# One linear-attention and two-MLP kernel: the product v_m · w per chunk in two half steps, the first chunk's by pairs of batches

## The chip, the core and the metric

The kernel runs on one core of a Trainium2 chip. The metric is the device time of one execution in microseconds (us). Three runs of the kernel before gave 841.07, 841.46 and 845.69 us, a median of 841.46 us.

## What is computed

Four batches of eight heads, 576 positions of 64 dimensions, go through an attention with 32 memory slots, and its output, 2304 rows of 512, through two MLPs:

```python
a = softmax(phi, over positions)               # (B, H, S, 32)
k_m, v_m = a^T k, a^T v                        # (B, H, 32, 64) each
attn = softmax(q k_m^T / 8, over the 32 slots) # (B, H, S, 32)
x = attn v_m                                   # as rows of 512
x = ((x w_a) * (x w_b)) w_out                  # first MLP, 1536 wide
out = elu(x w_in) w_out2                       # second MLP, 2048 wide
```

All data are 32-bit floats; the weights come as 64-bit floats and are turned into pairs of 32-bit parts on the chip.

## The kernel before, in words

**The parts hi and lo.** To keep accuracy, an operand is split into a part hi (rounded, written by ACT) and a part lo (the rest, subtracted by DVE). A product is three matmuls: hi·hi, hi·lo, lo·hi.

**v_m · w.** The kernel never forms x = attn v_m. It multiplies v_m by the first MLP's weights instead: for every chunk f of 128 of the 1536 columns, `step_u(f)` (L459) forms u = v_m·[w_a, w_b]. v_m stands in two tiles, `vthi` and `vtlo` (L254), of 128 partitions by 4 blocks `kc` of (batch, slot) columns. A head is half a column of the array, so two row tiles of 64 rows each (`i` = 0, 1) run side by side; each has its own PSUM tile `u_ps` of two banks. A chunk takes 4 blocks x 3 parts x 2 row tiles = 24 matmuls of 64x256. The columns of the result's partitions are the four batches' 32 slots: one pass gives u for all batches. Then ACT copies each PSUM tile into `ur` (`upper`, L482), DVE subtracts to get the lo part (`lower`, L485), and SP issues 16 transfers (L499) that spread `ur` over the four batches' own tiles `u`. The matmuls that use them are `ab_ps` (`steps_ab`, L617): attn's hi and lo parts `xhi`, `xlo` against u.

**The attention stage.** The loop over batches (L519) issues, for each batch b, in program order: `stage_kv(b, 0, ·)`, the k side (PSUM tile `pk`, L360), `stage_kT`, which copies it to `kt` (L374), `stage_scores(b)` (`sc`, `sl`, L390, L394), `stage_aT(b+1)`, the transposed softmax of the next batch (`tp_a`, L339), `stage_softmax(b)` (L416 to L420), `stage_kv(b, 1, 0)`, `stage_vT(b, 0)` (ACT copies into `vthi` at L380, DVE subtracts into `vtlo` at L382), `stage_norm(b)` (DVE L434 to L436, and a multiply on POOL at L438), `stage_kv(b, 1, 1)`, `stage_vT(b, 1)`. `stage_xT(b-1)` transposes the normalized scores into the PSUM tiles `tp_x` (L449) and `tl_x` (L453) and splits them into `xhi` (L69) and `xlo` (L70). In the last batch the v side goes first, then `stage_xT(2)`, then `step_u(0, 0)`, and only then the k side and the scores of batch 3.

**PSUM.** `pstile` (L61) hands out tiles of two banks from a pool of two during the attention stage; `sc`, `tp_a`, `tp_x` and `u_ps` take them in turn, so each waits until the tile before the last has been read. Later a second pool of two joins. `pone` gives single banks for `pk`, `tl_x` and `sl` from a pool of four.

**Order of the work.** All engines run their instructions in the order in which the program issues them. `step(pe, evac, amount)` (L218) issues one group of matmuls, then `fill(amount)`, then the evacuation, then what earlier steps have deferred by so many steps (`defer`). `fill` issues pieces of the weight conversion, seven DVE operations per unit of 128x512 weights (`piece`, L144: L155, L158, L142, L163, L168, L173, L176), with ACT operations between them (L113, L119, L133); a piece also issues the next unit's load on POOL's DMA queue (L103). SP issues the loads of q, k, v and phi and the 16 transfers of each chunk. Between the attention stage and the first MLP the kernel frees one pool of tiles and opens another; the softmax of batch 3 (L577 to L601) then runs beside the first `ab_ps` steps.

Of the kernel before, what the change touches and what calls it, by code (L numbers as in the profile page):

```python
# [7 lines left out]
F32 = mybir.dt.float32  # L8
F32R = mybir.dt.float32r
# [4 lines left out]
AF = mybir.ActivationFunctionType  # L14
ALU = mybir.AluOpType
# [6 lines left out]
def attention_then_two_mlps(ctx, tc, q, kv, kv_left, phi, w_ab, w_o1, w_i2, w_o2, out):  # L22
# [13 lines left out]
    nc = tc.nc  # L36
    B, P, KC, S = q.shape
# [23 lines left out]
    def pstile(name):  # L61
        turn[0] += 1
        return pss[turn[0] % len(pss)].tile([P, 2, 512], F32, tag="ps", name=name)
# [117 lines left out]
    def weights(key):  # L181

        n = index[key]
        while n in cu:
            assert piece(), key
        return ready[key]

    def drop(key):
        ready.pop(key)
        live[units[index[key]][1]] -= 1  # L190
# [3 lines left out]
    def fill(amount):  # L194
        credit[0] += amount
        while credit[0] >= 1.0:
            credit[0] -= 1.0
            if not piece():
                credit[0] = 0.0
# [10 lines left out]
    def defer(steps, fn, at=2):  # L210

        later.append([steps, fn, at])

    def flush_later():
        while later:
            later.pop(0)[1]()

    def step(pe, evac, amount, order=ORDER):  # L218


        pe()
        for e in later:
            e[0] -= 1
        due = [e for e in later if e[0] <= 0]
        later[:] = [e for e in later if e[0] > 0]
        evac = evac if isinstance(evac, list) else [evac]
        for k in order:
            if k == "f":
                fill(amount / order.count("f"))
            elif k in "abc":  # L230
                if "abc".index(k) < len(evac):
                    evac["abc".index(k)]()
            else:
                for e in due:
                    if e[2] == int(k):
                        e[1]()

    def tick():
        step(lambda: None, [], 0, "012")
# [5 lines left out]
    pu = es_u.enter_context(tc.tile_pool(name="pu", bufs=2, reuse_waits="tile"))  # L245
# [8 lines left out]
    vthi, vtlo = [pa.tile([P, KC, B, M], F32R, name=f"vt{x}") for x in ("hi", "lo")]  # L254
# [30 lines left out]
    for b in range(1, B):  # L285
        first, second = [("kv", b, 0, 0), ("kv", b, 0, 1), ("q", b, 0), ("q", b, 1)], [("kv", b, 1, 0), ("kv", b, 1, 1)]
        if b + 1 == B:
            first, second = second, first
# [63 lines left out]
    def stage_kv(b, n, u):  # L352

        a, t, left = st["a", b], st["kv", b, n, u], st["left", b]
        pk = pone("pk")
        for i in range(2):
            c = i if n == 0 or b % 2 == 0 else 1 - i
            for j in range(NJ + 1):
                rows = t[:, j, c, :] if j < NJ else left[0:LEFT, u, n, c, :]
                nc.tensor.matmul(pk[:, i * P:(i + 1) * P], rows, a[0:P if j < NJ else LEFT, u, j, :],  # L360
                                 start=(j == 0), stop=(j == NJ))
        st["pk", n, b, u] = pk
        more_loads("kv", *(("left",) if n == 1 and u == 1 else ()))

    def own(t, i, straight=True):

        if straight:
            return t[64 * i:64 * i + 64, 0:3 * P].rearrange("p (t s) -> p t s", s=192)[:, :, M * i:M * i + M]
        return t[64 * i:64 * i + 64, 64:192].rearrange("p (t s) -> p t s", s=64)[:, :, M * i:M * i + M]

    def stage_kT(b, u):
        pk = st.pop(("pk", 0, b, u))
        for i in range(2):
            nc.scalar.activation(out=own(kts[u], i), in_=own(pk, i), func=AF.Copy)  # L374

    def stage_vT(b, u):
        pk = st.pop(("pk", 1, b, u))
        hi, lo = [[x[64 * i:64 * i + 64, 2 * u:2 * u + 2, b, :] for i in range(2)] for x in (vthi, vtlo)]
        for i in range(2):
            nc.scalar.activation(out=hi[i], in_=own(pk, i, b % 2 == 0), func=AF.Copy)  # L380
        for i in range(2):
            nc.vector.tensor_tensor(out=lo[i], in0=own(pk, i, b % 2 == 0), in1=hi[i].bitcast(F32), op=ALU.subtract)  # L382
# [73 lines left out]

    u_t, g_t = {}, {}

    def step_u(f, amount):  # L459

        tiles = [pstile("u_ps") for _ in range(2)]

        def pe():
            for kc in range(KC):
                hi, lo = [x[:, (kc % 2) * 256:(kc % 2) * 256 + 256] for x in weights(("ab", f, kc // 2))]
                for n, (v, w) in enumerate(((vthi, hi), (vthi, lo), (vtlo, hi))):
                    for i in range(2):
                        r = slice(64 * i, 64 * i + 64)  # L470
                        nc.tensor.matmul(  # L471
                            tiles[i][:, kc // 2, (kc % 2) * 256:(kc % 2) * 256 + 256],
                            v[r, kc].rearrange("p b m -> p (b m)"), w[r], start=(n == 0), stop=(n == 2),
                        )
            drop(("ab", f, 0))
            drop(("ab", f, 1))

        us = [pu.tile([P, 2, 2, 256], F32R, tag="u", name="u", bufs=5) for _ in range(B)]
        ur = pu.tile([P, 2, KC, 2, 256], F32R, tag="ur", name="ur", bufs=1)

        def upper(i):
            nc.scalar.activation(out=ur[:, i, :, 0], in_=tiles[i].rearrange("p k (c n) -> p (k c) n", c=2), func=AF.Copy)  # L482

        def lower(i):
            nc.vector.tensor_tensor(out=ur[:, i, :, 1], in0=tiles[i].rearrange("p k (c n) -> p (k c) n", c=2),  # L485
                                    in1=ur[:, i, :, 0].bitcast(F32), op=ALU.subtract)

        def second():
            lower(0)
            upper(1)  # L490

        def third():
            lower(1)
            for b in range(B):
                for c in range(2):
                    for i in range(2):
                        o = 64 * c + M * i
                        src = ur[M * b:M * b + M, i].rearrange("p (k c) h n -> p k c (h n)", c=2)[:, :, c ^ (b % 2)]
                        nc.sync.dma_start(out=us[b][o:o + M].rearrange("p k h n -> p k (h n)").bitcast(F32),  # L499
                                          in_=src.bitcast(F32))  # L500

        defer(1, second)
        defer(2, third)
        for b in range(B):
            u_t[f, b] = us[b]
        step(pe, lambda: upper(0), amount)

    with tc.manual_schedule():
        make_identity(nc, ident)
        kts = [p0.tile([P, 3 * P], F32, name=f"kt{i}", bufs=1) for i in range(2)]  # L510
        for t in kts:
            nc.gpsimd.memset(t, 0.0)

        st["ident"] = ident
# [4 lines left out]
        for b in range(B):  # L519
            nxt = b + 1 < B  # L520
            if not nxt:
                stage_kv(b, 1, 0)
                stage_vT(b, 0)
                stage_kv(b, 1, 1)
                stage_vT(b, 1)
                flush_later()
                stage_xT(b - 1)
                step_u(0, 0)
            stage_kv(b, 0, 0)
            if b == 0:  # L530
                stage_kT(b, 0)
                stage_aT(0, (1,))
                stage_kv(b, 0, 1)
                stage_kT(b, 1)
                stage_a(1, 0)
                stage_a(1, 1)
            else:
                if nxt:
                    a_max(b + 1, 0)
                    a_max(b + 1, 1)  # L540
                stage_kT(b, 0)
                if nxt:
                    a_exp(b + 1, 0)
                stage_kv(b, 0, 1)
                stage_kT(b, 1)
                if nxt:
                    a_end(b + 1, 0)
                    a_exp(b + 1, 1)
                    a_end(b + 1, 1)
            if nxt:  # L550
                flush_later()
            else:
                tick()
            if nxt and b:
                stage_xT(b - 1)
            if b == 0:
                magnitude(0)
                low_word(0)
            else:
                fill(FA)  # L560
            stage_scores(b)
            if not nxt:
                tick()
                break
            stage_aT(b + 1)
            soft_tiles(b)
            stage_softmax(b)
            stage_kv(b, 1, 0)
            fill(FB)
            stage_vT(b, 0)  # L570
            stage_norm(b, nc.gpsimd)
            stage_kv(b, 1, 1)
            stage_vT(b, 1)
            fill(FC)


# [241 lines left out]
        for f in range(NF2):  # L818
            for k in range(NB):
                t = (f + k) % NB  # L820
# [63 lines left out]
```

## Time and profile before

| | |
|---|---|
| median of three runs | 841.46 us |
| the profiled execution | 842.81 us, span from first to last instruction 841.0 us |
| PE, matmuls | 818.8 us busy (97%), 5168 instructions |
| DVE | 612.7 us busy (73%), 1015 instructions |
| ACT | 415.0 us busy (49%), 646 instructions |
| POOL | 50.8 us busy (6%) |
| transfers u <- ur on SP's queue | 192, 128 KB each |

The span is the time from the first to the last instruction, and the run's own time contains what lies around it. PE is TensorE's matmuls, PEld its weight loads, DVE VectorE, ACT ScalarE, POOL GpSimd, SP SyncE. In the timelines each row gives start, duration, engine, line, operation, out <- in, count, and in square brackets the idle time of the engine before it with what ended it. Rows merge equal neighbours, so that a row's start is that of its first instruction.

### The profile page before, as it was taken

Reading aid. Unit: us, or ns where it says so; the run is one execution under the profiler, and the core shown is the slowest. Engines: PE = TensorE matmul, PEld = TensorE weight load, DVE = VectorE, ACT = ScalarE, POOL = GpSimd, SP = SyncE. Lnnn points to the kernel's source line nnn. Section 1 sums busy time; section 2 is a strip of 40 time slices with the busy share of each in tenths; the row PEclk is TensorE's granted clock in tenths of the full one; section 3 lists DMA queues with packets and bytes.
Section 4 is the critical chain, followed back from the end, with each engine's and each line's share of the span. In section 5 each row is a group of like instructions: output and inputs, shape, how many; then the busy total and the mean of one; then the engine's idle time right before and its main releaser. Section 6 shows DMA issues by size and latency. Waiting matters only on the chain.

```text
span 841.0 us, 13020 instructions
## 1 busy us (share of the span) xinstructions
PE 818.8 (97%) x5168; PEld 762.3 (91%) x5168; DVE 612.7 (73%) x1015; ACT 415.0 (49%) x646; POOL 50.8 (6%) x88
## 2 busy tenths in 40 slices
PE   5999988999999999999999999999999999999998
PEld 4887888999999999999999898889998889998896
DVE  1886688888997898567788852887777876776555
ACT  2544366664454544333348763565544565543360
POOL 1111200000000000000000000000000000000000
PEclk9998999999999999999999999999999999999999
DMA  9771566655765477416001110111111110100006
GB/s 308 280 272 55 126 151 173 173 136 138 161 157 134 111 175 156 113 55 151 29 2 50 51 51 1 51 51 51 51 51 51 51 50 26 51 26 1 1 0 225
DMA packets 32173, 82.90 MB, mean 99 GB/s; under 512 B 4849, under 2 KB 4849, under 8 KB 32113
## 3 DMA queue, kind: packets, MB, share of 16 engines
q1 hardware_dynamic: 22320, 46.41, 20.4%
q0 software_dynamic: 9792, 35.66, 14.5%
q8 instruction: 41, 0.67, 0.3%
q14 instruction: 20, 0.16, 0.1%
HBM read 52.17 MB, written 4.72 MB: 68 GB/s over the span
## 4 chain that ended last, share of the span: by engine, by line
PE 90%; DVE 5%; DMA 3%; ACT 1%; issue 1%; SPq 1%; DVEq 0%; ACTq 0%
PE o_ps L784 24%; PE h_ps L741 24%; PE o_ps L659 17%; PE ab_ps L617 15%; PE pk L360 5%; PE u_ps L471 2%; PE sc L390 1%; DVE ur L485 1%; DMA kv_t<-in_kv_dram 1%; DMA u<-ur 1%; DMA raw<-in_w_o_dram 1%; SPq L499 1%; DVE a_sb L626 1%; PE tp_a L339 0%; DVE gl L628 0%
## 5 line engine op out<-in xcount | busy, mean ns | idle before, releaser
L617 PE MATMUL ab_ps<-xhi,u 128*128 128x288 f32 x768 | 138.6, 297 | 2.9 <-DVE xlo L70 1.2
L617 PEld LDWEIGHTS ab_ps<-xhi,u 128*128 128x128 f32 x768 | 114.0, 188 | 4.8 <-DVE xlo L70 1.4
L784 PE MATMUL o_ps<-ulh,g2h 128*128 128x512 f32 x288 | 114.1, 396 | 0.0
L784 PE MATMUL o_ps<-ull,g2h 128*128 128x512 f32 x288 | 114.1, 396 | 0.0
L784 PE MATMUL o_ps<-ulh,g2l 128*128 128x512 f32 x288 | 103.4, 396 | 0.0
L759 DVE SCALAR_TENSOR_TENSOR e<-e,th 128x768 f32<-128x768 f32 x48 | 46.0, 959 | 76.2 <-ACT e L756 75.8
L741 PE MATMUL h_ps<-yh,usl 128*128 128x384 f32 x384 | 98.1, 336 | 0.0
L741 PE MATMUL h_ps<-yh,ush 128*128 128x384 f32 x384 | 98.1, 336 | 0.0
L741 PE MATMUL h_ps<-yl,ush 128*128 128x384 f32 x384 | 98.0, 336 | 0.0
L752 ACT ACTIVATE e<-h_ps 128x768 f32<-128x768 f32 x48 | 39.0, 813 | 96.0 <-PE h_ps L741 94.0
L659 PE MATMUL o_ps<-gh,ull 128*128 128x288 f32 x384 | 82.5, 296 | 0.9 <-DVE ull L142 0.9
L659 PE MATMUL o_ps<-gh,ulh 128*128 128x288 f32 x384 | 82.8, 297 | 0.1
L659 PE MATMUL o_ps<-gl,ulh 128*128 128x288 f32 x384 | 82.3, 295 | 0.0
L617 PE MATMUL ab_ps<-xlo,u 128*128 128x288 f32 x384 | 82.2, 296 | 0.0
L741 PEld LDWEIGHTS h_ps<-yh,ush 128*128 128x128 f32 x384 | 69.6, 188 | 1.3
L741 PEld LDWEIGHTS h_ps<-yh,usl 128*128 128x128 f32 x384 | 69.5, 188 | 0.0
L741 PEld LDWEIGHTS h_ps<-yl,ush 128*128 128x128 f32 x384 | 69.5, 188 | 0.0
L784 PEld LDWEIGHTS o_ps<-ulh,g2l 128*128 128x128 f32 x288 | 54.2, 188 | 13.2
L784 PEld LDWEIGHTS o_ps<-ulh,g2h 128*128 128x128 f32 x288 | 54.2, 188 | 12.5
L784 PEld LDWEIGHTS o_ps<-ull,g2h 128*128 128x128 f32 x288 | 54.2, 188 | 12.5
L626 DVE TENSOR_TENSOR a_sb<-a_sb,ab_ps 128x576 f32<-128x576 f32 x48 | 36.1, 752 | 36.5 <-PE ab_ps L617 30.6
L659 PEld LDWEIGHTS o_ps<-gh,ull 128*128 128x128 f32 x384 | 61.5, 188 | 1.1 <-DVE ull L142 1.1
(105 smaller groups left out, 1456.9 us busy)
## 6 DMA issues: line engine op xcount, KB each, us to landing
u<-ur SPq DMA_DIRECT2D x192, 128.0 KB, 4.5
raw<-in_w_o_dram POOLq DMA_DIRECT2D x28, 512.0 KB, 4.0
raw<-in_w_ab_dram POOLq DMA_DIRECT2D x24, 512.0 KB, 5.4
kv_t<-in_kv_dram SPq DMA_DIRECT2D x16, 512.0 KB, 6.6
raw<-in_w_i_dram POOLq DMA_DIRECT2D x16, 512.0 KB, 3.8
q_t<-in_q_dram SPq DMA_DIRECT2D x8, 576.0 KB, 7.2
out_dram<-y SPq DMA_DIRECT2D x8, 512.0 KB, 3.0
phi_t<-in_phi_dram SPq DMA_DIRECT2D x3, 576.0 KB, 4.8
```

Source lines behind the costliest of these rows:

```text
L360: nc.tensor.matmul(pk[:, i * P:(i + 1) * P], rows, a[0:P if j < NJ else LEFT, u, j, :], start=(j == 0), stop=(j == NJ))
L390: nc.tensor.matmul(sc[:, u, j * P:(j + 1) * P], qs[u][:, t, j * P:(j + 1) * P], kts[u][:, t * P:(t + 1) * P], start=(t == 0), stop=(t == 1))
L471: nc.tensor.matmul(tiles[i][:, kc // 2, (kc % 2) * 256:(kc % 2) * 256 + 256], v[r, kc].rearrange("p b m -> p (b m)"), w[r], start=(n == 0) ...
L485: nc.vector.tensor_tensor(out=ur[:, i, :, 1], in0=tiles[i].rearrange("p k (c n) -> p (k c) n", c=2), in1=ur[:, i, :, 0].bitcast(F32), op=A ...
L499: nc.sync.dma_start(out=us[b][o:o + M].rearrange("p k h n -> p k (h n)").bitcast(F32), in_=src.bitcast(F32))
L617: nc.tensor.matmul(ps[:, h, 0:HS], u[:, kk, w, n * P:n * P + P], x[b][:, kk, h * HS:(h + 1) * HS], start=(kk == 0 and i == 0), stop=(kk == ...
L626: nc.vector.tensor_tensor(out=a_sb, in0=a_sb, in1=ps[:, :, 0:HS], op=ALU.mult)
L659: nc.tensor.matmul(ps[:, h, 0:HS], w[:, cc], g[:, h * HS:(h + 1) * HS], start=(n == 0 and i == 0), stop=(n == len(fs) - 1 and i == 2),)
L741: nc.tensor.matmul(ps[:, h, 0:HB], w[:, c], x[:, c, h * HB:(h + 1) * HB], start=(c == 0 and i == 0), stop=(c == KC - 1 and i == 2),)
L752: nc.scalar.activation(out=e, in_=ps[:, :, 0:HB], func=AF.Relu, scale=-1.0)
L759: nc.vector.scalar_tensor_tensor(out=e, in0=e, scalar=1.0, in1=th, op0=ALU.add, op1=ALU.mult)
L784: nc.tensor.matmul(ps[:, k, :], g[:, c * P:(c + 1) * P], w, start=(f == fs[0] and i == 0), stop=(f == fs[-1] and i == 2),)
```

## The change

`step_u` takes a list of batches `bs` and does its work in two halves. Half k covers the weight unit k (blocks 2k and 2k+1) and has one PSUM tile, with row tile 0 in its first bank and row tile 1 in its second; its 12 matmuls, its copy to `ur` (128x1024, as before) and, one step later, its subtraction form a step of their own. The transfers follow the second half's subtraction. The first chunk is done twice: for batches 0 and 1 at the end of batch 2's turn, with a `tick()` that issues the second subtraction and the 8 transfers at once, and for batches 2 and 3 at the old place. Each of the two calls issues all 24 matmuls, over all 128 partitions. `vthi` and `vtlo` are cleared at the start on POOL, since batch 3's columns are not yet written at the first call.

```diff
-    def step_u(f, amount):
-        tiles = [pstile("u_ps") for _ in range(2)]
-        def pe():
-            for kc in range(KC):
-                hi, lo = [x[:, (kc % 2) * 256:(kc % 2) * 256 + 256] for x in weights(("ab", f, kc // 2))]
-                for n, (v, w) in enumerate(((vthi, hi), (vthi, lo), (vtlo, hi))):
-                    for i in range(2):
-                        r = slice(64 * i, 64 * i + 64)
-                        nc.tensor.matmul(
-                            tiles[i][:, kc // 2, (kc % 2) * 256:(kc % 2) * 256 + 256],
-                            v[r, kc].rearrange("p b m -> p (b m)"), w[r], start=(n == 0), stop=(n == 2),
-                        )
-            drop(("ab", f, 0))
-            drop(("ab", f, 1))
...
-        def second():
-            lower(0)
-            upper(1)
-        def third():
-            lower(1)
-            for b in range(B):
...
-        defer(1, second)
-        defer(2, third)
-        for b in range(B):
-            u_t[f, b] = us[b]
-        step(pe, lambda: upper(0), amount)
+    def step_u(f, amount, bs=tuple(range(B))):
+        us = {b: pu.tile([P, 2, 2, 256], F32R, tag="u", name="u", bufs=5) for b in bs}
         ur = pu.tile([P, 2, KC, 2, 256], F32R, tag="ur", name="ur", bufs=1)
+        u_t.update({(f, b): us[b] for b in bs})
+        def half(k):
+            ps = pstile("u_ps")
+            def pe():
+                whi, wlo = weights(("ab", f, k))
+                for c in range(2):
+                    for n, (v, w) in enumerate(((vthi, whi), (vthi, wlo), (vtlo, whi))):
+                        for i in range(2):
+                            r = slice(64 * i, 64 * i + 64)
+                            nc.tensor.matmul(
+                                ps[:, i, c * 256:c * 256 + 256], v[r, 2 * k + c].rearrange("p b m -> p (b m)"),
+                                w[r, c * 256:c * 256 + 256], start=(n == 0), stop=(n == 2),
+                            )
+                if bs[-1] == B - 1:
+                    drop(("ab", f, k))
+            src = ps.rearrange("p i (c n) -> p i c n", c=2)
+            hi, lo = [ur[:, :, 2 * k:2 * k + 2, x] for x in range(2)]
+            def lower():
+                nc.vector.tensor_tensor(out=lo, in0=src, in1=hi.bitcast(F32), op=ALU.subtract)
+                if k == 1:
+                    spread()
+            step(pe, lambda: nc.scalar.activation(out=hi, in_=src, func=AF.Copy), amount / 2)
+            defer(1, lower)
+        def spread():
+            for b in bs:
...
+        half(0)
+        half(1)
...
-        for t in kts:
+        for t in kts + [x.bitcast(F32) for x in (vthi, vtlo)]:
             nc.gpsimd.memset(t, 0.0)
...
                 stage_xT(b - 1)
-                step_u(0, 0)
+                step_u(0, 0, (2, 3))
...
             stage_vT(b, 1)
+            if b == B - 2:
+                step_u(0, 0, (0, 1))
+                tick()
             fill(FC)
```

## Rows read from the trace of the kernel before

**Rows 1.** Busy us by engine (count), granted clock and DMA share in four stretches.
```profile
79.72:86.54 6.82, 6.58 (x37) 5.91 (x38) 3.15 (x5) 1.94 (x2) 0.00 (x0) 0.50 0.02 4
...
95.00:158.00 63.00, 55.34 (x438) 52.94 (x436) 55.41 (x97) 39.94 (x80) 7.22 (x11) 1.00 0.55 140
158.00:840.00 682.00, 678.81 (x4160) 635.98 (x4160) 500.00 (x808) 337.51 (x480) 30.65 (x55) 1.00 0.29 78
```
**Rows 2.** Timeline of PE, 70 to 80 us.
```profile
70.48 1.16 PE L360 MATMUL pk<-a_t,kv_t 128*128 128x128 f32 x8
...
76.50 1.09 PE L449 MATMUL tp_x<-ident,at 128*128 128x128 f32 x8
...
77.67 0.36 PE L471 MATMUL u_ps<-ush,vthi 64*128 64x256 f32 x1
...
79.96 0.58 PE L471 MATMUL u_ps<-ush,vthi 64*128 64x256 f32 x1 [1.94 <-DVE xlo L70]
```
**Rows 3.** Timeline of PE, 82 to 96 us.
```profile
82.82 2.07 PE L360 MATMUL pk<-a_t,kv_t 128*128 128x128 f32 x8
...
87.51 1.16 PE L360 MATMUL pk<-a_t,kv_t 128*128 128x128 f32 x8
...
90.52 3.84 PE L390 MATMUL sc<-kt,q_t 128*128 128x128 f32 x32
...
95.31 0.53 PE L617 MATMUL ab_ps<-xhi,u 128*128 128x288 f32 x2
```
**Rows 4.** Timeline of DVE, 94 to 158 us.
```profile
94.40 1.23 DVE L416 TENSOR_REDUCE small<-sc 128x32 f32<-128x1024 f32 x1 [6.74 <-PE sc L390]
...
131.67 1.23 DVE L485 TENSOR_TENSOR ur<-u_ps,ur 128x1024 fp32r<-128x1024 f32 x1 [1.41 <-ACT ur L482]
```
**Rows 5.** Timeline of PE, 150 to 152 us: first u matmuls of a later chunk, and what follows.
```profile
150.00 0.39 PE L471 MATMUL u_ps<-ush,vthi 64*128 64x256 f32 x2
...
151.63 0.53 PE L617 MATMUL ab_ps<-xhi,u 128*128 128x288 f32 x2
```
**Rows 6.** Timeline of DVE and POOL, 60 to 78 us.
```profile
61.77 0.68 DVE L142 TENSOR_TENSOR usl<-a,ush 128x512 fp32r<-128x512 f32 x1
...
71.06 1.90 POOL L438 TENSOR_TENSOR at<-at,ssm 128x1024 f32<-128x1024 f32 x1 [6.87 <-ACT vthi L380]
71.18 1.81 DVE L435 TENSOR_SCALAR ssm<-ssm 64x8 f32<-64x8 f32 x1
...
73.25 0.46 DVE L382 TENSOR_TENSOR vtlo<-pk,vthi 64x64 fp32r<-64x64 f32 x2
```
**Rows 7.** Evacuations and transfers of u: ns min/median/max, and us to landing.
```profile
L482 ACT ACTIVATE ur<-u_ps x24: 1016/1022/1037, 82.7 to 376.7; 128x1024 fp32r<-128x1024 f32 x24
L485 DVE TENSOR_TENSOR ur<-u_ps,ur x24: 1215/1218/1226, 83.8 to 378.4; 128x1024 fp32r<-128x1024 f32 x24
...
L499 SPq DMA_DIRECT2D u<-ur x192: 585/595/1708, 85.0 to 388.8; - x192
...
DMA to landing us min/median/max: 2.3/4.5/7.9
```
**Rows 8.** Timeline of ACT and POOL, 87 to 91 us.
```profile
87.28 0.59 POOL L103 DMA_DIRECT2D raw<-in_w_ab_dram  x1 [13.28 <-issue]
...
87.62 0.45 ACT L374 ACTIVATE kt<-pk 64x64 f32<-64x64 f32 x2 [2.96 <-PE pk L360]
```
**Rows 9.** Timeline of PE, 104 to 117 us: the two longest waits before ab matmuls.
```profile
108.16 0.53 PE L617 MATMUL ab_ps<-xhi,u 128*128 128x288 f32 x2 [1.21 <-DVE xlo L70]
...
116.00 0.50 PE L617 MATMUL ab_ps<-xhi,u 128*128 128x288 f32 x2 [1.20 <-DMA u<-ur]
```
**Rows 10.** Timeline of all engines, 0 to 10 us.
```profile
1.26 0.77 POOL L512 MEMSET kt<- 128x384 f32 x2
...
8.44 0.26 ACT L346 ACTIVATE a_t<-tl_a 64x128 f32<-64x128 f32 x1
...
9.27 2.05 PE L360 MATMUL pk<-a_t,kv_t 128*128 128x128 f32 x8 [1.15 <-DMA kv_t<-in_kv_dram]
```

More of the change, by code (lines that the diff above doesn't have):

```diff
@@ L457, in attention_then_two_mlps @@
     u_t, g_t = {}, {}
-    def step_u(f, amount):
-        tiles = [pstile("u_ps") for _ in range(2)]
-        def pe():
-            for kc in range(KC):
-                hi, lo = [x[:, (kc % 2) * 256:(kc % 2) * 256 + 256] for x in weights(("ab", f, kc // 2))]
-                for n, (v, w) in enumerate(((vthi, hi), (vthi, lo), (vtlo, hi))):
-                    for i in range(2):
-                        r = slice(64 * i, 64 * i + 64)
-                        nc.tensor.matmul(
-                            tiles[i][:, kc // 2, (kc % 2) * 256:(kc % 2) * 256 + 256],
-                            v[r, kc].rearrange("p b m -> p (b m)"), w[r], start=(n == 0), stop=(n == 2),
-                        )
-            drop(("ab", f, 0))
-            drop(("ab", f, 1))
-        us = [pu.tile([P, 2, 2, 256], F32R, tag="u", name="u", bufs=5) for _ in range(B)]
-        ur = pu.tile([P, 2, KC, 2, 256], F32R, tag="ur", name="ur", bufs=1)
[L481 to L486, printed above, removed]
-        def second():
-            lower(0)
-            upper(1)
-        def third():
-            lower(1)
-            for b in range(B):
```

## The prediction

> **What bounds the kernel now.** I read the page's engine shares first, then the busy times by stretch, then the timelines of the stretch that the change touches. From 158 us on PE is busy 678.8 of 682 us [rows 1]: nothing there can be won but PE's own work, and eight of the eleven later chunks lie there. From 95 to 158 us DVE is busy 55.4 of 63 us and PE 55.3 [rows 1]: PE waits there for DVE's weight conversion, and DVE's chain begins when the last scores are done, at 94.40, after 6.74 us with nothing to do [rows 4]. So whatever delays PE on its way to the end of batch 3's scores delays DVE's chain, and through it everything behind, by the same amount. What matters is the stretch from 70 us to 95.31, where the first `ab_ps` matmul starts [rows 3].
>
> In that stretch PE is bound by itself but for one wait: `tp_x` starts at 76.50, one u matmul goes at 77.67, the second row tile's needs the bank pair that `tp_x` holds, and PE stands 1.94 us until `xlo` has read it, at 79.96 [rows 2]. From 79.72 to 86.54 the granted clock is 0.50, which is 1.2 GHz; before and after it is 2.4 GHz [rows 1]. Eight `pk` matmuls that take 1.16 us at 87.51 take 2.07 us at 82.82 [rows 3].
>
> **The first chunk, at the new place.** The new call stands where PE ends batch 2's v side and begins batch 3's, at 70.48 [rows 2].
> - *Work added.* 24 matmuls, the length of a chunk: from 150.00 to 151.63 a later chunk takes 1.63 us, 0.068 us each [rows 5]. They compute all batches' columns again, since a pass over 128 columns costs the same for two batches as for four. PE gains nothing from the halving: **+1.6 us**.
> - *A new wait.* The first half needs blocks 0 and 1, whose `vtlo` is long done, and weights that were converted by 62.5 us [rows 6]; its tile was last that of batch 2's scores, long read by their softmax. It runs from 70.48 to 71.30. The second half's first four matmuls use `vthi` alone (71.57). The fifth needs `vtlo` of blocks 2 and 3. DVE writes that only at 73.25 to 73.71, since the norm stands before it in program order, in it an operation of 1.81 us on 64x8 that ends with POOL's multiply of 1.90 us beside it [rows 6]. PE waits from 71.57 to about 73.75: **+2.2 us**. Nothing in the change moves the norm, so I take this value. Its ends are 0, if that DVE operation were not late, and 3.3, if the wait stood before the first matmul. Behind PE's wait stand batch 3's v side, its transposes and its scores, so all of it counts.
>
> **The first chunk, at the old place.** `tp_x` now starts 3.9 us later, at about 80.4. The first half has a tile to itself, so 12 matmuls run while `xlo` is awaited instead of one: 11 x 0.068 = **-0.75 us**; PE's wait shrinks from 1.94 to about 1.2 us. It is 0 at worst.
>
> **Beside the path.** The copies cost as much as before per call, 2 x 1.02 on ACT and 2 x 1.22 on DVE [rows 7], so one call more is +2.0 and +2.4 us. On DVE they fall at 73.7 to 76.7, and the four conversion pieces behind them end at 79.1; `xlo` comes at 82.6, so they stay covered. The first 8 transfers go out at 76.8, 0.6 us apart [rows 7], the last at 81.3, and land after 2.3 to 7.9 us, median 4.5 [rows 7]: about 86. The second call's copies write the one `ur` that these transfers read, so ACT stands until then, and its copies end at about 88. Behind them stands `kt`'s copy, which waits for PE anyway: `pk` of batch 3 is now done at 87.8, 0.2 us after the 87.62 of before [rows 8]. I put this at nothing; at the longest landing, 7.9 us, ACT would be free at 91.2 and the scores 0.9 us late. On DVE the second subtraction moves to about 89.7, and the conversion pieces behind it, with the load that POOL issued at 87.28 [rows 8], some 3 us later: the 6.74 us of idle time [rows 4] cover that. The last 8 transfers then land by 100 us, and batch 2's `ab_ps` start at 108.16 [rows 9]. SP has no loads left to hold up. That batches 0 and 1 have u sooner wins nothing: at 95.31 PE started them straight after the scores [rows 3].
>
> **The clock.** Between 79.96 and 87.51 PE did 23 u matmuls and one `pk` group of 20 [rows 2, 3]. At 2.4 GHz these are 1.56 us and 3.01 (87.51 to 90.52 [rows 3]), together 4.57 against 7.55: the low clock cost 3.0 us. Half of the 6.58 us of PE time in the low stretch, 3.3, says the same [rows 1]. What PE did before the fall: 1.2 us of transposes, one matmul, 1.94 us of standing [rows 2]. With the change 12 matmuls stand between the transposes and a shorter wait. Elsewhere PE stood 1.21 and 1.20 us between ab or u matmuls and the clock stayed [rows 1, 9]. I take no fall at the old place: **-3.0 us**; at worst 0. The new wait, 2.2 us, is longer than the one before the fall but has multiplies right before and behind it; its worst is another +3.0.
>
> The Trainium skill's page "TensorE: Matmul & The Clock Gate" (Part 4: PE-mode transpose) says that transposes do not count as PE-busy in the way that other matmuls do. By that rule the fall belonged to transposes and wait together, and the new wait alone would cost no clock (841.6); if transposes count, a wait of 2.2 us is by itself enough, and that is the first or second rival below. No row here decides it.
>
> **The start.** Two clears of 128x512 take 0.77 x 512/384 = 1.0 us on POOL [rows 10], and the first two weight loads go out so much later. `kv_t` may land earlier for it: PE waited for it until 9.27, with its other operand ready at 8.70 [rows 10]. So 0 to -0.6; I take **-0.2**, nearer to nothing, since the loads of q and phi still share the engines.
>
> **Later chunks.** The same matmuls, copies and transfers, in two steps instead of one. An extra step brings what earlier steps deferred one place forward: a `gl` subtraction now precedes the first u subtraction. Where DVE waited 1.41 us for ACT's copy [rows 4], the copy of the first half comes 0.5 us sooner and the `gl` fills the rest; the second subtraction ends where it did or 0.3 later. PE's waits for a second u tile shrink by up to 0.75 each, but DVE ends last there. I take **+0.2**, between +0.5 and -1.2, the last if the transfer wait before 116.00 went [rows 9].
>
> **The sum**: 1.6 + 2.2 - 0.75 - 3.0 - 0.2 + 0.2 = +0.1 us. On the profiled execution, 842.81, this is 842.9; that execution stood 1.35 above the median of 841.46, so I predict **841.6 us**.
>
> **The rivals.**
> - *One fall again* (at the old or at the new place): +3.0, 844.6 us. For it: a wait of over a microsecond at each place; against: 0.75 us of matmuls more at the old one. Still under half a per cent.
> - *Slower: both waits cost the clock.* The new wait pulls it down from about 74 us and the old one again from about 84, each for some 6.8 us as in rows 1: +6.0, 847.6 us (+0.7%). It decides from the second fall on. For it: 2.2 us is more than the 1.94 after which it fell. Against: dense `pk` matmuls on both sides.
> - *Faster: the new wait does not come* (DVE reaches `vtlo` by 71.5) and the start gives its whole 0.6: 841.6 - 2.2 - 0.4 = 839.0 us. Against it: the same DVE order. Even so it is 0.3%.
> - *The change doesn't do what it says it does*: the halving saves no matmul, because the columns are computed for all four batches both times. This is in the sum already.
>
> **How the numbers follow.** About 0.5% (4.2 us) is what a measurement of this kernel can tell from no change: 837.3 to 845.7. Chances: the forecast 0.48, one fall 0.33, both falls 0.10, faster 0.09. The forecast's case with its ends (start, later chunks, ur) lies between 840 and 843.5, one fall at 843.5 to 846. The range from 839.0 to 846.6 holds these and leaves out the second fall and half of the gains, some 0.16. Slower by over 0.5%: the second fall's 0.10 and the top of one fall, 0.05, make 0.15. Faster by over 0.5%: more than any case gives, 0.06 for what I don't see in 95 to 158 us. The rest, 0.79, is no change.
>
> **What would show it.** In the changed trace: 24 u matmuls from about 70.5, with a wait of 2.2 us behind the sixteenth that ends with `vtlo`; `tp_x` at 80.4; 12 u matmuls before a wait of some 1.2 us; clock at 1.00 from there on; the first `ab_ps` at about 95.4; ACT's third u copy held by transfers until about 86; no new PE idle after 158. I am wrong if the first `ab_ps` moves by over 3 us either way, if the clock falls twice, or if the time between it and 158 changes by over a microsecond.

## The result, and the profile after

The changed kernel takes **847.73 us** (median of 10 runs, 844.54 to 849.40); the kernel before, in 10 runs beside it, 842.45 (840.81 to 845.88). The ratio is 1.0053 with the interval 1.0031 to 1.0074: slower by half a per cent, 6.1 us above the predicted 841.6 and 1.1 us above the range. The profiled execution took 849.09 us, its span 847.3 at a mean granted clock of 0.989 (before: 842.81, 841.0, 0.996).

Three marks on PE cut the span in the same places in every kernel: **M0**, the first `pk` group of batch 2's v side; **M1**, the first `ab_ps` matmul; **M2**, the first `o_ps` matmul behind the last weight conversion that PE waits for, behind which it is busy to the end. Before, they stand at 64.57, 95.31 [rows 3] and 158.08 us; after, at 62.39, 99.39 and 164.43.

| us | to M0 | M0 to M1 | M1 to M2 | M2 to end |
|---|---|---|---|---|
| before | 64.57 | 30.74 | 62.77 | 682.94 |
| changed | 62.39 | 37.00 | 65.04 | 682.90 |
| difference | -2.18 | +6.26 | +2.27 | -0.04 |

The busy times by stretch of the changed kernel, for two stretches of low granted clock and two long ones (columns as in [rows 1]):

```profile
71.19:84.85 13.66, 13.47 (x54) 11.46 (x55) 5.66 (x12) 2.53 (x6) 0.61 (x1) 0.50 0.34 78
112.15:115.57 3.42, 3.33 (x14) 3.34 (x15) 3.39 (x7) 1.93 (x4) 0.59 (x1) 0.50 0.29 57
99.00:162.00 63.00, 55.40 (x429) 53.02 (x428) 53.27 (x93) 39.82 (x80) 7.21 (x11) 0.97 0.50 127
162.00:846.00 684.00, 680.27 (x4172) 637.25 (x4170) 502.48 (x811) 337.71 (x480) 30.74 (x55) 1.00 0.29 78
```

The one low stretch of before, 6.82 us [rows 1], is now 13.66 us, and a second one of 3.42 us stands in the stretch behind the scores, which had none. The last row is as before: PE still has nothing between its matmuls.

The timeline of PE in the changed kernel, from M0 to the first waits behind M1:

```profile
62.39 1.06 PE L360 MATMUL pk<-a_t,kv_t 128*128 128x128 f32 x8
...
69.04 0.38 PE L476 MATMUL u_ps<-usl,vthi 64*128 64x256 f32 x2
71.38 0.84 PE L476 MATMUL u_ps<-ush,vtlo 64*128 64x256 f32 x2 [1.96 <-DVE vtlo L382]
...
72.78 2.07 PE L360 MATMUL pk<-a_t,kv_t 128*128 128x128 f32 x8
...
83.69 1.62 PE L449 MATMUL tp_x<-ident,at 128*128 128x128 f32 x8
...
87.69 0.39 PE L476 MATMUL u_ps<-ush,vthi 64*128 64x256 f32 x2 [1.34 <-DVE xlo L70]
...
88.59 1.16 PE L360 MATMUL pk<-a_t,kv_t 128*128 128x128 f32 x8
...
99.39 0.53 PE L618 MATMUL ab_ps<-xhi,u 128*128 128x288 f32 x2
...
112.24 0.85 PE L618 MATMUL ab_ps<-xhi,u 128*128 128x288 f32 x2 [1.91 <-DVE xlo L70]
```

The new wait is there, behind the sixteenth u matmul, from 69.42 to 71.38 us, and ends with `vtlo`. The clock falls in it: the matmuls behind it take 0.84 us where a pair takes 0.38, and the `pk` groups of batch 3's v side 2.07 us each, where [rows 2, 3] have 1.16. It is back when the old wait comes (87.69), and that one costs 1.34 us and no clock.

The timeline of DVE in the changed kernel, at the new wait and at the last scores:

```profile
69.03 1.81 DVE L435 TENSOR_SCALAR ssm<-ssm 64x8 f32<-64x8 f32 x1
...
71.10 0.48 DVE L382 TENSOR_TENSOR vtlo<-pk,vthi 64x64 fp32r<-64x64 f32 x2
...
98.48 1.22 DVE L416 TENSOR_REDUCE small<-sc 128x32 f32<-128x1024 f32 x1 [5.98 <-PE sc L390]
```

The operation of 1.81 us stands ahead of `vtlo` as in [rows 6], and before the last scores' reduction DVE still has 5.98 us of idle time [rows 4: 6.74]: the added evacuations are hidden.

### The profile page after: what moved, and what is told of

Same layout as the page of the kernel before. It is cut to its first block, busy times and chain, and to the rows that moved or that the text cites. A ratio compares the mean times of both kernels' runs of the same rounds, so it can differ in the third digit from the quotient of the medians.

```text
span 847.3 us, 13062 instructions
## 1 busy us (share of the span) xinstructions
PE 823.3 (97%) x5192; PEld 766.1 (90%) x5192; DVE 615.1 (73%) x1017; ACT 417.1 (49%) x648; POOL 51.8 (6%) x90
## 4 chain that ended last, share of the span: by engine, by line
PE 90%; DVE 5%; DMA 2%; ACT 2%; issue 1%; SPq 0%; DVEq 0%; ACTq 0%
PE o_ps L785 24%; PE h_ps L742 24%; PE o_ps L660 17%; PE ab_ps L618 14%; PE pk L360 6%; PE u_ps L476 2%; PE sc L390 2%; DMA raw<-in_w_o_dram 1%; DVE ur L487 1%; PE tp_a L339 1%; DVE a_sb L627 1%; DVE a L176 0%; DMA raw<-in_w_ab_dram 0%; PE tp_x L449 0%; DMA phi_t<-in_phi_dram 0%
## 5 line engine op out<-in xcount | busy, mean ns | idle before, releaser
L660 PEld LDWEIGHTS o_ps<-gh,ulh 128*128 128x128 f32 x384 | 61.5, 188 | 0.9 <-PE o_ps L660 0.3
```

The costliest lines, as they stand in the source:

```text
L660: nc.tensor.matmul(ps[:, h, 0:HS], w[:, cc], g[:, h * HS:(h + 1) * HS], start=(n == 0 and i == 0), stop=(n == len(fs) - 1 and i == 2),)
```

## The experiments

The theory: the wait for `vtlo` takes the clock down, and that is most of the loss. Rivals: the half steps cost it; the added 24 matmuls and 8 transfers cost it without any clock; the old place keeps its fall. All kernels, by the marks of their profile, with the low stretches behind M0 (start, length), and, where a kernel was timed in several runs, the ratio of its time to that of the kernel before, which ran beside it on the same chip. The ratio is not the quotient of the two medians and differs from it by up to 0.003; the medians of the kernel before were 843.33 us beside e1 to e4, 843.89 beside e5 to e8, 843.58 beside e9 to e12 and 842.12 beside e13 to e15.

| kernel | M0 | M0-M1 | M1-M2 | low clock | ratio |
|---|---|---|---|---|---|
| before | 64.6 | 30.7 | 62.8 | 79.7 (6.8) | |
| changed | 62.4 | 37.0 | 65.0 | 71.2 (13.7), 112.1 (3.4) | 1.0053 |
| e9 changed, again | 61.1 | 35.7 | 66.1 | 72.0 (10.2), 109.5 (3.4) | 1.0074 |
| e1 halves only | 67.6 | 27.2 | 64.7 | 106.8 (6.8) | 0.9982 |
| e4 pairs only | 61.2 | 37.9 | 64.3 | 72.1 (10.2), 85.7, 109.6, 133.5 (3.4 each) | 1.0099 |
| e2 wait removed | 62.0 | 32.8 | 64.6 | 80.7 (6.8), 108.0 (3.4) | 1.0030 |
| e3 wait filled | 65.4 | 33.7 | 64.4 | 99.0 (3.4) | 1.0032 |
| e5 filled in place | 66.0 | 31.1 | 65.4 | 111.0 (3.4) | 1.0005 |
| e8 pairs, no waits | 61.1 | 27.8 | 66.9 | 102.6, 143.6 (3.4 each) | 0.9984 |
| e10 old wait filled | 64.0 | 28.0 | 65.6 | 104.6 (3.4), 125.1 (6.8) | 0.9996 |
| e13 clears only | 63.4 | 32.4 | 63.4 | 80.1 (10.2) | 1.0000 |
| e14 clears, again | 63.9 | 30.9 | 63.7 | 80.8 (6.8), 104.7, 128.6 (3.4 each) | |
| e6 u behind k | 65.2 | 28.1 | 64.3 | 94.1 (3.4), 124.8 (6.8) | 0.9964 |
| e7 e6 in halves | 68.1 | 29.0 | 63.7 | 97.2 (3.4) | 0.9984 |
| e11 u first | 64.7 | 25.8 | 63.5 | 100.3, 124.2 (3.4 each) | 0.9959 |
| e12 e11 in halves | 63.9 | 25.8 | 63.9 | 103.3 (3.4) | 0.9968 |
| e15 e11 and clears | 61.2 | 25.8 | 63.6 | 99.3, 119.8 (3.4 each) | 0.9960 |

From M2 to the end each takes 682.90 to 683.10 us.

**e1, the half steps alone.** The changed kernel with the first chunk done once, and without the clears:

```diff
-                step_u(0, 0, (2, 3))
+                step_u(0, 0)
...
-            if b == B - 2:
-                step_u(0, 0, (0, 1))
-                tick()
```

> The two half steps without the pairs: one call of the first chunk at the old place, no clears, every chunk still in halves. Theory A (the clock and the new place cost the time, the halving does not): the new wait and the 24 extra matmuls are gone, 1.6 + 2.0 us, and the clock has only the old wait, about 1.2 us long, to fall at; 839 us if it stays at 2.4 GHz there, 842 us if it falls, so 0 to 4 us faster than before. Theory B (the half steps themselves slow the later chunks between 95 and 160 us): 844 to 846 us, 2 to 3 us slower than before.

843.18 us, ratio 0.9982 (0.9956 to 1.0008): no loss. PE's timeline at the old place:

```profile
79.51 1.10 PE L449 MATMUL tp_x<-ident,at 128*128 128x128 f32 x8
...
82.98 0.39 PE L476 MATMUL u_ps<-ush,vthi 64*128 64x256 f32 x2 [1.34 <-DVE xlo L70]
...
83.89 1.16 PE L360 MATMUL pk<-a_t,kv_t 128*128 128x128 f32 x8
...
107.53 0.85 PE L615 MATMUL ab_ps<-xhi,u 128*128 128x288 f32 x2 [1.91 <-DVE xlo L70]
```

The wait shrank from 1.94 to 1.34 us and the clock held: M0 to M1 is 3.57 us shorter, where the prediction's two terms for this place give 3.75. But the fall came later, at 106.8, in a wait of 1.91 us where [rows 9] has 1.21. In the step ahead of it PE's waits were 1.03 and 1.21 us before; in halves they are 0.43 and 1.91: the sum hardly changes, since DVE ends both, but the one wait is longer.

**e4, the pairs alone.** The step of before with a list of batches, the clears and the two calls; no halves:

```diff
-    def step_u(f, amount):
+    def step_u(f, amount, bs=tuple(range(B))):
...
-                step_u(0, 0)
+                step_u(0, 0, (2, 3))
...
+            if b == B - 2:
+                step_u(0, 0, (0, 1))
+                tick()
```

> The pairs without the halves: the first chunk done twice, with the step of before (two PSUM tiles, one step), and vthi and vtlo cleared. Theory A (the new place carries the loss): the same wait of 2.0 us and the same fall at the new place, the old wait back to 1.9 us; 848 to 849 us. Theory B (the halves carry it): 843 to 845 us, for the 24 extra matmuls and a part of the wait alone.

851.59 us, 1.0099 (1.0061 to 1.0138), above what either theory gave. PE's timeline:

```profile
70.20 0.64 PE L471 MATMUL u_ps<-ush,vtlo 64*128 64x256 f32 x2 [1.95 <-DVE vtlo L382]
...
73.03 2.07 PE L360 MATMUL pk<-a_t,kv_t 128*128 128x128 f32 x8
...
85.18 0.38 PE L471 MATMUL u_ps<-ush,vthi 64*128 64x256 f32 x1 [1.93 <-DVE xlo L70]
```

Here the clock fell behind both waits, at 72.1, 1.9 us after the first had ended, and at 85.7. The pairs carry the whole loss. That the halves take some of it back, by the shorter second wait, fits the lower ratio of the changed kernel, but the intervals overlap.

**e9, the changed kernel again**, unaltered, with more runs beside it.

> The changed kernel once more, beside the three below and the kernel before on one chip, to compare all of them there. Theory A (the new wait takes the clock down in most executions, for longer than the old one did): 847 to 848 us, 4 to 5 us over before, a mean granted clock of about 0.993, and a fall at 71 us in the profile. Theory B (the first measurement was high by chance): 844 us.

848.91 us, 1.0074 (1.0042 to 1.0106). The same wait is there, and the clock falls at 72.0, 1.9 us after its end:

```profile
70.10 0.64 PE L476 MATMUL u_ps<-ush,vtlo 64*128 64x256 f32 x2 [1.95 <-DVE vtlo L382]
...
85.09 0.39 PE L476 MATMUL u_ps<-ush,vthi 64*128 64x256 f32 x2 [1.34 <-DVE xlo L70]
...
109.64 0.85 PE L618 MATMUL ab_ps<-xhi,u 128*128 128x288 f32 x2 [1.91 <-DVE xlo L70]
```

**e2, the new wait removed.** Batch 2's norm goes behind its `vtlo`:

```diff
-            stage_norm(b, nc.gpsimd)
+            if b != B - 2:
+                stage_norm(b, nc.gpsimd)
...
             if b == B - 2:
+                stage_norm(b, nc.gpsimd)
                 step_u(0, 0, (0, 1))
```

> The changed kernel with batch 2's norm moved behind its second v subtraction, so that the new wait for vtlo has nothing to wait for. Theory A (that wait of 2.0 us, and above all the half clock of 13.7 us after it, carry the loss): no stop at the new place and no fall there; 2.0 us of wait and 3 to 6 us of clock back, 841 to 843 us. Theory B (the clock falls anyway, at the old wait): only the 2.0 us come back, 845.7 us.

844.96 us (841.79 to 852.68 in 12 runs), 1.0030 (0.9999 to 1.0061): between the two theories and nearer to B. PE no longer waits among the first 24 matmuls, and nothing falls at 71 us. In this profile the clock fell at the old place instead:

```profile
80.02 0.39 PE L476 MATMUL u_ps<-ush,vthi 64*128 64x256 f32 x2 [1.28 <-DVE xlo L70]
...
81.03 2.08 PE L360 MATMUL pk<-a_t,kv_t 128*128 128x128 f32 x8
```

The changed kernel, e9, e1, e3 and e5 did not fall at a wait of 1.34 or 1.35 us in that place, this one did at 1.28: a wait of this length goes either way. So this run alone does not tell the theories apart; e5 does.

**e3 and e5, the new wait filled.** 18 spare 128x256 matmuls stand where PE waits. In e5 they write the second half's own tile ahead of its matmuls (in e3, a bank of another pool ahead of the first `vtlo` matmul):

```diff
                 whi, wlo = weights(("ab", f, k))
+                for _ in range(18 if k == 1 and bs == (0, 1) else 0):
+                    nc.tensor.matmul(ps[:, 0, 0:256], vthi[:, 0].rearrange("p b m -> p (b m)"), whi[:, 0:256],
+                                     start=True, stop=True)
```

> The changed kernel, with 18 spare matmuls of 128x256 (1.9 us at 2.4 GHz) whose result nobody reads put into the new wait: PE is as late as before, but never stands there. Theory A (standing still takes the clock down): no fall at 71 us, at most one at the old wait; 3 to 6 us faster than the changed kernel, 842 to 845 us. Theory B (the wait's length counts, not the clock): 847.7 us, as the changed kernel.

> The changed kernel with the same 18 spare matmuls in the new wait, this time written into the second half's own PSUM tile before its real matmuls, so that no bank of the rotation is taken (the first filled run showed a wait of 2.5 us before the first ab matmul that the spare bank may have made). Theory A (standing still takes the clock down; the work added and the wait itself are worth about 3 us): no fall at the new place, no wait before the first ab matmul, 842.5 to 844.5 us. Theory B (the halves' order in the later chunks costs as much as the clock): the first ab matmul comes as theory A says, but the stretch behind it stays 2 us longer than before.

e3: 845.52 us, 1.0032 (1.0009 to 1.0056); PE stood 2.51 us before M1, for nothing that the profile names, and the clock fell there. The spare bank may be the reason; e5 repeats the run without it and has no such wait. e5: 845.23 us, **1.0005** (0.9988 to 1.0023). Its busy times, then PE's timeline:

```profile
64.00:96.00 32.00, 30.65 (x246) 26.77 (x245) 19.71 (x34) 13.13 (x27) 4.21 (x6) 1.00 0.43 112
```
```profile
72.62 2.41 PE L473 MATMUL u_ps<-ush,vthi 128*128 128x256 f32 x18
...
75.92 1.16 PE L360 MATMUL pk<-a_t,kv_t 128*128 128x128 f32 x8
```

PE spends as long at this place as in the changed kernel, 2.41 us of spare work for 1.96 of waiting, and does everything else the same. The clock holds, M0 to M1 is 31.11 us against 37.00 and 35.68 in the changed kernel's two profiles, and no loss is left that can be told from noise. This is the direct test of the theory: what the wait costs above its own length is the clock. M1 to M2 is 65.4 us as in the changed kernel, 2.6 longer than before: theory B's sign is there too, so this part of the loss is not the new wait's.

**e8, pairs with no wait on either side.** e2, and the second call moved behind batch 3's first k-side product:

```diff
-                step_u(0, 0, (2, 3))
                 stage_kv(b, 0, 0)
+            if not nxt:
+                step_u(0, 0, (2, 3))
```

> The changed kernel with both of its waits covered: batch 2's norm behind its second v subtraction, and the second call behind batch 3's first k-side product. Theory A (the waits and their half clock make the loss): 2.0 + 1.3 us of waits and 3 to 6 us of clock less than the changed kernel, first ab matmul about 3 us earlier than before by the clock and the old wait, less 1.6 us for the extra matmuls: 840 to 842 us. Theory B (the extra work has another cost): 844 us or more.

842.56 us, 0.9984 (0.9960 to 1.0009), just above what theory A gave. M0 to M1 is 27.84 us, 2.9 under before although it holds the 24 extra matmuls; M1 to M2 is 66.93, 4.2 above. The timelines of ACT and DVE show two waits:

```profile
81.79 1.94 ACT L491 ACTIVATE ur<-u_ps 128x1024 fp32r<-128x1024 f32 x2 [3.83 <-DMA u<-ur]
...
141.94 0.65 ACT L119 ACTIVATE lw<-raw 128x512 bf16<-128x512 uint32 x1 [5.12 <-DMA raw<-in_w_o_dram]
143.83 0.43 DVE L155 TENSOR_SCALAR a<-a 128x512 f32<-128x512 f32 x1 [4.02 <-ACT a L113]
```

The first is the predicted hold of the second call's copies by the first call's transfers. The second is new: a weight load, issued by POOL at 134.39, came in only at 141.94, and PE, which had stood 2.01 us, fell to the low clock at 143.6.

**e10, the old wait filled**, on the kernel before, with the same 18 matmuls between the transposes and the u matmuls; and **e13, e14, the clears alone** (twice the same kernel):

```diff
         def pe():
+            for _ in range(18 if f == 0 else 0):
+                nc.tensor.matmul(tiles[0][:, 0, 0:256], vthi[:, 0].rearrange("p b m -> p (b m)"),
+                                 weights(("ab", 0, 0))[0][:, 0:256], start=True, stop=True)
```
```diff
-        for t in kts:
+        for t in kts + [x.bitcast(F32) for x in (vthi, vtlo)]:
```

> The kernel before with 18 spare matmuls of 128x256 in its own wait for xlo, written into the first row tile's PSUM tile before the real ones: the same wait in length, but PE doesn't stand. Theory A (the 1.94 us of standing cost 3.0 us by the clock in the kernel before): no fall at 80 us, T from the start of batch 2's v side to the first ab matmul 27.8 us instead of 30.7; 839 to 841 us. Theory B (the transposes or the batch's other work take the clock down, not the wait): the fall stays, 843 to 844 us, as before.

> The kernel before with nothing of the change but the two clears of vthi and vtlo on POOL at the start, which send the first two weight loads out some 1 us later. In the seven kernels with the clears so far PE did not wait for kv_t (before the first pk matmuls), in the seven without it waited 0.8 to 2.2 us; the start of the first pk matmul of batch 2's v side lay at 62.7 us on the mean of the seven with, 65.4 without. If the clears do it: no kv_t wait, that mark between 61 and 64, the first rise of the clock between 10 and 14, and a ratio of 0.996 to 0.999. If it is only the spread of the first rise, which has nothing to do with the clears: the wait is gone, the first pk starts 0.4 us earlier, the mark lies anywhere between 61 and 68, and the ratio is 0.9985 to 1.0015.

> The same kernel once more, for a second look at the start, since the mark varies from run to run. If the clears do it: again no kv_t wait and the mark between 61 and 64; if not, anywhere between 61 and 68.

e10: 841.62 us, 0.9996 (0.9970 to 1.0021), between the two theories by time. The fall at the old place is gone, as theory A said, in its busy times:

```profile
64.00:92.00 28.00, 28.00 (x215) 24.31 (x213) 16.60 (x31) 11.14 (x25) 3.62 (x5) 1.00 0.32 92
104.55:107.97 3.42, 3.14 (x13) 3.14 (x14) 3.39 (x7) 2.08 (x3) 0.59 (x1) 0.51 0.19 41
125.10:131.90 6.80, 6.16 (x37) 5.94 (x38) 5.02 (x8) 4.94 (x10) 0.58 (x1) 0.50 0.38 121
```

But the 2.8 us won before M1 were given back behind it (M1 to M2 is 2.9 us longer), with two falls there. (Its profile's clock, 0.993, is lower than the 0.9960 of its 12 runs on the mean.) e13: 844.30 us, 1.0000 (0.9976 to 1.0025), e14: 843.22 in one run. PE's wait for `kv_t` is gone in both and M0 stands at 63.4 and 63.9, but no gain shows in the time. In e13 the same code as before fell for 10.2 us at the old place, not 6.8.

**A better place: e6, e7, e11, e12, e15.** e6 moves the whole step of before behind batch 3's first k-side product; e11 moves it ahead of batch 2's transposes, with that product behind it and a `tick()` that issues its deferred subtraction there:

```diff
-                stage_xT(b - 1)
                 step_u(0, 0)
                 stage_kv(b, 0, 0)
+            if not nxt:
+                tick()
+                stage_xT(b - 1)
```

e7 and e12 are these with the half steps of e1, and e15 is e11 with the two clears.

> The kernel before with one move: the first chunk's u behind batch 3's first k-side product, so that 3.0 us of pk matmuls stand where PE waited 1.94 us for xlo. No pairs, no halves. Theory A (that wait takes the clock down in the kernel before, too): no wait, no fall at 80 us, scores done 4 to 5 us earlier; u's transfers start 2 to 3 us later, which may cost up to 2 us before the first ab matmul: 839 to 841 us, 2 to 4 us faster than before. Theory B (the clock falls for another reason): 841.5 us, the wait alone.

> The same move with the half steps, without the pairs. Theory A: as the move alone between the scores and the first ab matmul; if the half steps cost 2 us in the stretch behind it, 841 to 843 us. Theory B (the half steps cost nothing there): 839 to 841 us, as the move alone.

> The kernel before with the first chunk's u in front of batch 2's transposes instead of behind them, batch 3's first k-side product between the two, and the deferred subtraction issued behind that product: nothing stands between u and its operands, and tp_x finds its tile read. No pairs, no halves. Theory A (both the old wait and its fall can go at no cost): first ab matmul 25.8 us after batch 2's v side began instead of 30.7, transfers in time, 838 to 840 us, the fastest so far. Theory B (a new wait takes the place of the old): 841 us or more.

> The same order with the half steps. Theory A (the half steps' only cost is the longer wait for xlo in the second chunk, 1.9 us instead of 1.2, where the clock then falls): as the run without halves up to the first ab matmul, then 1 to 2 us more in the stretch to the last wait of PE: 839.5 to 842 us. Theory B (the half steps cost nothing): the same time as without them.

> The fastest kernel so far (u before batch 2's transposes, 0.9959) with the same two clears. If they shorten the start by 1 to 3 us on the mean: 0.992 to 0.995, about 837 us where the kernel before has 843. If the start only varies: 0.995 to 0.9975, as without them. The stretch from the mark to the first ab matmul stays at 25.8 us either way.

e6: 842.38 us, 0.9964 (0.9942 to 0.9985). e7: 842.55, 0.9984 (0.9958 to 1.0009). In both PE stands before M1 for the u transfers, which now leave later, 2.54 and 3.48 us:

```profile
93.27 0.50 PE L618 MATMUL ab_ps<-xhi,u 128*128 128x288 f32 x2 [2.54 <-DMA u<-ur]
```

e11: **838.21 us, 0.9959** (0.9937 to 0.9981); e12: 839.36, 0.9968 (0.9943 to 0.9994); e15: 839.06, 0.9960 (0.9936 to 0.9984). e11's busy times from M0 to M1, then PE's waits (what for; us, times, longest):

```profile
64.72:90.53 25.81, 25.81 (x197) 22.30 (x195) 16.59 (x31) 11.01 (x25) 3.62 (x5) 1.00 0.39 111
```
```profile
PE u_ps L471 <- ACT y L669: 2.1, 1, 2.1
PE pk L360 <- DMA kv_t<-in_kv_dram: 1.2, 1, 1.2
PE u_ps L471 <- DVE a_sb L628: 1.0, 1, 1.0
PE ab_ps L619 <- DMA u<-ur: 1.0, 1, 1.0
```

From M0 to M1 PE stands nowhere and the clock is full: the first chunk's wait for `xlo` is covered by work that had to be done anyway. The second chunk's wait for `xlo`, 1.21 us in [rows 9], is not among e11's waits either, but there the clock had fallen just before, at 100.3; in e15 it is back with 1.20 us. The intervals of e6, e11, e12 and e15 lie below 1: these four beat both kernels. e15 against e11 shows again that the clears win no time.

## Why the prediction was wrong

**The steps that held.** The added matmuls, the new wait (2.2 predicted, 1.96 measured, behind the sixteenth matmul, for `vtlo`, with the norm ahead of it on DVE), the shorter old wait (1.2, measured 1.34), the hidden evacuations, SP's and POOL's nothing, and no new idle time behind M2. The hold of ACT by transfers did not show in the changed kernel, since the low clock made PE later than the transfers: the third copy ran as soon as PE had written it. It shows in e8.

**The step that failed: "I take no fall at the old place: -3.0 us", with no fall at the new one.** The old place's half of it held (it did not fall there in either profile of the changed kernel, nor in e1; it did in e2). The new place's half did not: the wait of 1.96 us took the clock down, and for longer than [rows 1], 13.66 us and in e9 10.2. The prediction gave such a fall a price of 3.0 and had it lasting 6.8 us. PE was busy 13.47 us of the 13.66 at half speed, so the fall cost 13.47 / 2 = 6.7 us; the old one cost 6.58 / 2 = 3.3. With it the sum closes: 1.63 for the matmuls, 1.96 for the new wait, 1.94 - 1.34 = 0.60 less at the old one, 6.7 - 3.3 = 3.4 for the clock, together +6.4 by this estimate from one profile each; measured from M0 to M1, +6.26. e5 shows it from the other side: the wait filled, the clock holds and M0 to M1 is back at 31.11. The first `ab_ps` moved by 4.08 us, one of the prediction's own signs of being wrong.

**Which rival came.** "Both waits cost the clock" gave 847.6, and the time was 847.73, but that is luck: its mechanism was not what happened, which was one long fall at the new place and one in the next chunk, none at the old. "One fall again" named the place rightly and had the size, 3.0, at less than half of the profile's 6.7.

The prediction's sentence from the Trainium skill, page "TensorE: Matmul & The Clock Gate" (Part 4: PE-mode transpose), made the new wait free of clock (841.6). The changed kernel's trace speaks against reading it so: no transpose stands between M0 and the new wait, `pk` and u matmuls lie on both sides, and the clock fell at 71.19.

**The second term that was mis-sized: later chunks, +0.2, between +0.5 and -1.2.** M1 to M2 grew by 2.27 us, in e9 by 3.28. The fall at 112.1 is 3.33 / 2 = 1.7 of it, at the wait for `xlo` that the half steps lengthened to 1.91 us (e1 and e9 have it too). The prediction took PE's waits in that stretch for waits on the weight conversion; of before's, only the last is one (0.87 us, at M2), and the longest are for `xlo` and for u's transfers [rows 9]. What the half steps cost by themselves is not settled: e1 shows no loss, and e11 against e12 (0.9959 and 0.9968) have intervals that overlap.

**The start, -0.2.** The wait for `kv_t` went, as said; M0 came 2.18 us earlier mostly for another reason, a shorter slow start of PE (below). The clears alone give 1.0000; a gain of over 2 us by them is outside that interval, a smaller one is not.

**What was wrong in the method.** The 3.0 us that the old fall cost were read from one profile and counted as if they could be won. The granted clocks of all runs say more. (1 - clock) x span is an estimate of what the low clock took from a run, on the mean of a series:

| series | runs | mean clock | (1 - clock) x span, us |
|---|---|---|---|
| before, beside e1 | 29 | 0.9936 | 5.4 |
| e1, halves only | 12 | 0.9973 | 2.2 |
| changed, first series | 10 | 0.9931 | 5.8 |
| before, beside e9 | 31 | 0.9939 | 5.1 |
| e9, changed again | 8 | 0.9918 | 7.0 |
| e5, filled in place | 12 | 0.9981 | 1.6 |

The kernel before has 0.996 in its profile (3.4 us), so its other runs fall more; the changed kernel has 0.989 in its first profile, as low as any of its ten. So the shorter old wait did give back the 3 us that the prediction took (e1 against before), and the new wait took 3.6 to 4.8 again (changed against e1, which ran in another series). Against the kernel before, that leaves the clock only 1.9 of the 5.8 us between e9's two means (848.99 and 843.17), less than the two profiles suggest; 3.9 are the added matmuls, the waits and the later chunks, which the prediction put at 3.05 (1.6 + 2.2 - 0.75 - 0.2 + 0.2) and expected the clock to pay for. The changed kernel's executions show both parts: seven of 18 had a clock of 0.989 and took 848.52 to 854.37 us, three had 0.998 and took 844.54 to 846.70, still more than before.

Nor does a microsecond of this estimate cost a microsecond of time: over the 286 executions of the series with several runs, each set against the mean of its own series, one more goes with about 0.6 more. Where e10 took the fall away, the time stayed: all kernels but before and e13 fall somewhere between 94 and 113 us in their profile. A fall avoided at one wait can come at a later one.

## What to carry to other kernels

Doing a product a second time for half of its columns costs all of its matmuls again; it pays only where these fill time that would be idle, and the wait that it was to fill has to be looked for at the new place as well, in the program order of the engine that writes its operands (here a norm stood ahead of `vtlo`). A wait of 2 us on PE among dense matmuls is to be priced with the clock: here it cost its 2 us and some 4 to 7 more (3.6 to 4.8 on the mean of the runs, 6.7 in one profile). What cures such a wait is independent work that is due anyway, put between the producer and the consumer (e11), at no extra matmul; and a loss of clock read from one profile should be held against the granted clocks of all runs before it is counted as a gain.

## What the runs showed of the hardware that was not expected

**PE starts at half pace for a time that varies.** PE's timeline at the start of the changed kernel and of e1:

```profile
8.84 2.07 PE L360 MATMUL pk<-a_t,kv_t 128*128 128x128 f32 x8 [0.47 <-ACT a_t L343]
...
15.15 1.16 PE L360 MATMUL pk<-a_t,kv_t 128*128 128x128 f32 x8 [0.58 <-ACT a_t L343]
```
```profile
19.29 2.07 PE L360 MATMUL pk<-a_t,kv_t 128*128 128x128 f32 x8
```

In e4 and e9 the second group, at 11.1 and 11.0 us, already takes 1.16 us; in e1 the fourth still takes 2.07. These are the times that the same group takes at a granted clock of 1.00 and of 0.50. But the record of the granted clock does not show it: it reads 1.00 over the whole start, as in these busy times of the kernel before, whose first groups also take 2.07 us:

```profile
8.00:30.00 22.00, 20.38 (x123) 17.65 (x123) 8.76 (x20) 9.17 (x22) 0.00 (x0) 1.00 0.96 333
```

So that this is the clock's first rise is inferred from the times alone, and the mean clocks above leave it out. M0 follows, from 61.1 to 68.1 us, a spread of 7 us where runs of one kernel differ by 10 (before: 836.83 to 846.73 in 31 runs). The cause of the late rise was not found.

**A fall lasts differently.** The same code at the same wait fell for 6.8 us (before, e14) and for 10.2 (e13), the changed kernel's for 13.7 and 10.2; others lasted 3.4.

**A weight load beside the u transfers can be late.** The 512 KB load that e8 issued at 134.39 was awaited by ACT until 141.94; in before the same load, issued at 139.89, was awaited until 145.24. Whether the transfers beside it made the difference was not tried.
